# Attention with column norms and a soft mixture of experts: five products of ones in place of nine, a first load in three parts, and a new order of all steps

## The chip, the cores and the metric

The kernel runs on one core of one Trainium2 chip. The metric is device time in microseconds (us), the median of several runs. The engines are named as in the profile: PE is TensorE (PEld its weight loads), DVE is VectorE, ACT is ScalarE, POOL is GpSimd, SP is SyncE, which issues all loads and stores here.

## The reference, cut to what matters

```python
B, N, C = 4, 5056, 256                      # q, k, v: [B, N, C], float32
qn = q / (norm(q, axis=1) + 1e-6)           # a norm for each column, over the N rows
kn = k / (norm(k, axis=1) + 1e-6)
s = kn.transpose(0, 2, 1) @ qn / tau        # [B, C, C]: channels by channels
a = softmax(s, -1)
x = (v @ a).reshape(B * N, C)               # 20224 rows
logits = x @ phi                            # 8 experts of 4 slots: 32 columns
d = softmax(logits, 0)                      # over all 20224 rows
slot_in = d.T @ x                           # [32, C]
slot_out[e] = relu(slot_in[e] @ w1[e]) @ w2[e]   # F = 1024
out = softmax(logits, 1) @ slot_out         # [20224, C]
```

## The kernel before

The work comes in 40 units of 512 rows of q and k (`raw0` to `raw39`, ten for a batch, each one load of 1 MB by `load_qk`), 20 pairs of row blocks of v (`v0` to `v19`, five for a batch, 1 MB each), and the weights.

For each unit, PE sums k^T q of its four row blocks (j = 0 to 3, 128 rows each) into a bank of PSUM, `S0` to `S3` for the four batches (`score`, line 255). A half of a unit (two of the four blocks) is done in one of two ways. Plain, it is four products with float32 operands; the trace records a float32 product as two pieces, so that these are eight records, with the operand named `raw`. Split, if it stands in the table `SPLIT`, ACT first makes a rounded copy (`cast`, line 204), DVE the rest that the rounding left (`low`, line 209), both into a buffer `hl<unit>_<half>`, and PE does twelve quicker products on these. Of each row block the first product needs the cast alone, the second the rest too. For the norms ACT squares each unit (`square`, line 220) and DVE adds the squares up (`add`, line 235).

When a batch is summed, its norms and its softmax are worked out and folded with phi into a matrix `M<batch>`. Logits `L<pair>` (line 403) are products of v, turned so that channels lie on the partitions, with M. Turned v (`x<pair>`, two halves by channel) is either loaded turned from a second copy in memory (`load_vt`; the pairs and halves of the table `LT`), or made by PE from v (`turn`, line 376, into a bank `vTp<pair>_<block>_<half>`) and copied by ACT (`turned`, line 381). `G` (line 503) gathers v by the weights of the dispatch softmax. All this is interleaved with the later units' sums.

After the last unit comes a tail: the slots' inputs are joined over batches (`gs`, `gt`, `slp`, lines 518 to 621), the experts run (`H`, line 677; a transposition `hTp`, line 693, copied to `hT`; `O`, line 711), and each output block is a product (`op`, line 750) of the flipped softmax weights (`lg`, flipped by DVE, line 651) with the slots' outputs, copied out of PSUM by ACT and DVE (lines 772 and 774) and stored in 25 stores.

The order of all this is written out by hand: the program first makes a list of 992 steps and then emits them in the order of the table `ORDER`. Every engine does its instructions in the order of emission. Big buffers are 22 places of SBUF, assigned by the table `HOME`; a load into a place waits until its last reader is done.

At the very start DVE writes a tile of ones, and PE multiplies it with itself `WAKE` times (`wake`, line 787), ahead of its first product on loaded data; each is two records. The first load is line 167.

Of the kernel before, what the change touches and what calls it, by code (L numbers as in the profile page):

```python
# [20 lines left out]
WAKE = 9  # L21
PITCH = 128
NU = B * UB
NRAW = 5
MIX = (UB - 1, 3 * UB - 1)
SPLIT = {(u, 0) for u in range(1, NU) if u not in (1, 2, 3, 17, 20, 27, 31)} | {(u, 1) for u in (2, 5, 14, 24, 26, 27, 31, 33, 35, 37, 39)}
LT = {(p, 0) for p in (0, 2, 3, 4, 5, 6, 7, 8, 9, 11, 12, 13, 15, 18, 19)} | {(p, 1) for p in (0, 3, 6, 9, 12, 15)}
GR = {b: (3, 2) for b in range(B)}
HOME = {
# [74 lines left out]
def colnorm_attention_soft_moe(  # L104
# [59 lines left out]
    def load_few():  # L164
        sp.dma_start(few_sb, few)

    load_qk(0, ((0, 1), (1, 4)))
    for u in range(1, NRAW):
        load_qk(u)

# [623 lines left out]

    at(-2, wake, WAKE)
    FV = 13
    for u in range(NU):
# [3 lines left out]
        for k in range(2):  # L801
            if (u, k) in SPLIT:
                at(u - 1.08, cast, u, k)
# [292 lines left out]
```

## Time and profile before

| | |
|---|---|
| median of 3 runs | 277.36 us (277.16 to 277.69) |
| profiled execution, its own time | 277.06 us |
| its span in the trace | 275.3 us |
| PE busy | 254.6 us, 92% of the span |
| DVE busy | 236.8 us, 86% |
| ACT busy | 195.5 us, 71% |
| moved by the DMA queues | 111.44 MB, of them 20.97 MB written |

The span is what the profiler saw between the first and the last instruction; 1.76 us of the execution's own time lie outside it. The shares are averages over three different stages: the units (to about 200 us), the join and the experts (to about 217 us), and the output.

### The profile page before, as it was taken

The numbers are of one execution on the slowest core, as the hardware profiler recorded it, in microseconds if no ns is written. First come the engines' busy times: TensorE is split into PE (matmuls) and PEld (weight loads), VectorE is DVE, ScalarE is ACT, GpSimd is POOL, SyncE is SP. The second block draws the span as 40 slices with busy tenths as digits, with TensorE's granted clock in tenths as the row PEclk, the third lists the DMA queues.
The fourth block names the chain that finished last, engine by engine and source line by source line (L and its number), as shares of the span: only waits on it lengthen the run. The fifth ranks groups of instructions, "written<-read, shape, count | busy, mean of one in ns | idle before, by whom it ended". The sixth has DMA issues, their size and how long they took to land.

```text
span 275.3 us, 6127 instructions
## 1 busy us (share of the span) xinstructions
PE 254.6 (92%) x2494; PEld 212.6 (77%) x2494; DVE 236.8 (86%) x349; ACT 195.5 (71%) x285; POOL 7.5 (3%) x12
## 2 busy tenths in 40 slices
PE   8999999999999999999999999999999988678730
PEld 8889998999998896997898978866555878457520
DVE  1599999999999999999999997887989879988630
ACT  3898989798899689899998783886416247353430
POOL 1000002000002000020000001000000000000000
PEclk9999999999999999999999999999999999855755
DMA  7999999999999999999999999999999789999995
GB/s 283 432 424 410 422 426 415 420 417 419 419 417 420 412 422 421 416 415 417 412 419 418 416 417 419 417 416 420 421 415 420 300 332 388 418 418 412 420 421 246
DMA packets 17883, 111.44 MB, mean 405 GB/s; under 512 B 2112, under 2 KB 2112, under 8 KB 6592
## 3 DMA queue, kind: packets, MB, share of 16 engines
q1 hardware_dynamic: 17856, 111.06, 98.0%
q8 instruction: 19, 0.31, 0.4%
q14 instruction: 8, 0.07, 0.1%
HBM read 90.08 MB, written 20.97 MB: 403 GB/s over the span
## 4 chain that ended last, share of the span: by engine, by line
PE 87%; DVE 6%; ACT 3%; issue 1%; DVEq 0%; ACTq 0%
PE S L255 46%; PE op_None L750 8%; PE L L403 7%; PE G L503 7%; PE vTp L376 6%; PE op L750 3%; PE O L711 2%; DVE o L774 2%; ACT o L772 2%; PE wake L787 2%; PE Mp L347 1%; PE nn L266 1%; DVE nat L630 1%; DVE cm L627 1%; PE sp L549 1%; PE gt L525 1%
## 5 line engine op out<-in xcount | busy, mean ns | idle before, releaser
L235 DVE TENSOR_TENSOR sq<-sq,sq 128x1024 f32<-128x1024 f32 (+1 forms) x61 | 81.3, 1356 | 8.4 <-ACT sq L220 8.0
L220 ACT ACTIVATE sq<-raw 128x2048 f32<-128x2048 f32 (+1 forms) x40 | 74.7, 1889 | 6.5 <-DMA raw<-in_qk_dram 4.8
L255 PE MATMUL S<-hl 128*128 128x256 f32 x516 | 71.5, 291 | 0.0
L255 PE MATMUL S<-raw 128*128 128x256 f32 (+1 forms) x296 | 66.9, 384 | 0.0
L255 PEld LDWEIGHTS S<-hl 128*128 128x128 f32 x516 | 65.2, 191 | 1.0
L255 PEld LDWEIGHTS S<-raw 128*128 128x128 f32 (+1 forms) x296 | 53.7, 192 | 8.1 <-issue 1.5
L209 DVE TENSOR_TENSOR hl<-raw,hl 128x1024 fp32r<-128x1024 f32 x43 | 51.6, 1219 | 0.7 <-ACT hl L204 0.7
L204 ACT CAST hl<-raw 128x1024 fp32r<-128x1024 f32 x43 | 44.0, 1048 | 6.1 <-PE S L255 2.5
L750 PE MATMUL op_None<-so,lg 32*128 32x256 f32 x240 | 26.4, 525 | 6.0 <-ACT o L772 4.1
L772 ACT COPY o<-op_None 128x512 f32<-128x512 f32 x30 | 15.8, 594 | 18.2 <-PE op_None L750 17.9
L750 PEld LDWEIGHTS op_None<-so,lg 32*128 32x128 f32 x240 | 19.6, 251 | 11.6 <-ACT o L772 6.3
L381 ACT COPY x<-vTp 128x512 f32<-128x512 f32 x38 | 21.5, 593 | 9.3 <-PE vTp L376 8.8
L774 DVE COPY o<-op_None 128x512 f32<-128x512 f32 x30 | 19.0, 678 | 8.0 <-PE op_None L750 8.0
L376 PE MATMUL vTp<-ident,v 128*128 128x128 f32 x152 | 21.6, 276 | 0.0
L403 PE MATMUL L<-x,M 128*32 128x256 f32 (+1 forms) x320 | 20.3, 379 | 0.0
L376 PEld LDWEIGHTS vTp<-ident,v 128*128 128x128 f32 x152 | 17.3, 143 | 2.8 <-issue 2.5
L503 PE MATMUL G<-v,dn 128*32 128x256 f32 x320 | 19.1, 381 | 0.0
L503 PEld LDWEIGHTS G<-v,dn 128*32 128x32 f32 x320 | 10.8, 110 | 5.9 <-issue 0.7
L403 PEld LDWEIGHTS L<-x,M 128*32 128x32 f32 x320 | 9.8, 109 | 6.2 <-issue 0.8
L750 PE MATMUL op<-so,lg 32*128 32x128 f32 x160 | 9.6, 315 | 2.0 <-ACT o L772 1.4
L750 PEld LDWEIGHTS op<-so,lg 32*128 32x128 f32 x160 | 7.7, 197 | 4.4 <-ACT o L772 2.7
L772 ACT COPY o<-op 128x256 f32<-128x256 f32 x20 | 6.4, 378 | 6.3 <-PE op L750 6.3
(112 smaller groups left out, 233.0 us busy)
## 6 DMA issues: line engine op xcount, KB each, us to landing
raw<-in_qk_dram SPq DMA_DIRECT2D x37, 1024.0 KB, 12.5
v<-in_v_dram SPq DMA_DIRECT2D x20, 1024.0 KB, 11.1
w<-in_moe_w_dram SPq DMA_DIRECT2D x16, 1024.0 KB, 17.5
out_dram<-o SPq DMA_DIRECT2D x15, 1024.0 KB, 7.5
x<-in_vt_dram SPq DMA_DIRECT2D x17, 512.0 KB, 10.2
out_dram<-o SPq DMA_DIRECT2D x10, 512.0 KB, 3.7
raw<-in_qk_dram SPq DMA_DIRECT2D x3, 768.0 KB, 10.0
x<-in_vt_dram SPq DMA_DIRECT2D x4, 480.0 KB, 11.9
```

Source lines behind the costliest of these rows:

```text
L204: act.copy(hl[:, :, 0::2, :], raws[u][:, 2 * k : 2 * k + 2])
L209: dve.tensor_tensor(hl[:, :, 1::2, :], raws[u][:, 2 * k : 2 * k + 2], hl[:, :, 0::2, :].bitcast(F32), op=ALU.subtract)
L220: act.activation(sq_tile(u)[:, :n], raws[u][:, :n], AF.Square)
L235: dve.tensor_tensor(a[:, lo:hi], a[:, lo:hi], s[:, lo:hi], op=ALU.add)
L255: pe.matmul(sm, w, x, start=first[bb], stop=False, skip_group_check=True)
L376: pe.transpose(tp[:, P * jj : P * jj + P], vs[p][:, 4 * h + jj, P * m : P * m + P], ident)
L381: act.copy(x[:, h * UT : h * UT + UT], tps[p, h, m])
L403: pe.matmul(L[S * g : S * g + S, :n, :], M[:, m, :], x[:, :n, S * g : S * g + S], start=m == 0, stop=m == 1,)
L503: pe.matmul(gp[S * g : S * g + S, :C], dn[:, x, j, :], vt[:, j, :], start=x == 0 and j < G, stop=x == n - 1 and j >= G,)
L750: pe.matmul(ops[b, p, hf, g][:, h, :], cT[b][S * g : S * g + S, 4 * i : 4 * i + 4, :].rearrange("s j t -> s (j t)"), so[S * g : S * g + S] ...
L772: act.copy(dst, src)
L774: dve.tensor_copy(dst, src)
```

## The change

`WAKE` goes from 9 to 5. The first load, unit 0, comes in three parts (block 0, block 1, blocks 2 and 3) in place of two (block 0, blocks 1 to 3). The table `SPLIT` has 41 halves in place of 43: six are gone (the second half of unit 5, the first halves of units 4, 13, 22, 23 and 25), four are new (the first halves of units 1 and 31, the second halves of units 19 and 25). In `LT` the first channel half of pair 1 is now loaded turned, and that of pair 18 is turned on PE. `HOME` and `ORDER` are new throughout. The program's text is otherwise the same; its line numbers are lower by one from line 100 on.

```diff
-WAKE = 9
+WAKE = 5
...
-SPLIT = {(u, 0) for u in range(1, NU) if u not in (1, 2, 3, 17, 20, 27, 31)} | {(u, 1) for u in (2, 5, 14, 24, 26, 27, 31, 33, 35, 37, 39)}
-LT = {(p, 0) for p in (0, 2, 3, 4, 5, 6, 7, 8, 9, 11, 12, 13, 15, 18, 19)} | {(p, 1) for p in (0, 3, 6, 9, 12, 15)}
+SPLIT = {(u, 0) for u in range(1, NU) if u not in (2, 3, 4, 13, 17, 20, 22, 23, 25, 27)} | {(u, 1) for u in (2, 14, 19, 24, 25, 26, 27, 31, 33, 35, 37, 39)}
+LT = {(p, 0) for p in (0, 1, 2, 3, 4, 5, 6, 7, 8, 9, 11, 12, 13, 15, 19)} | {(p, 1) for p in (0, 3, 6, 9, 12, 15)}
...
-    "raw0": 0, "raw1": 1, "raw2": 2, "raw3": 3, "raw4": 4, "sq0": 5, "sq1": 6, "sq2": 8, "hl2_1": 7, "sq3": 18,
...
+    "raw0": 0, "raw1": 1, "raw2": 2, "raw3": 3, "raw4": 4, "sq0": 5, "sq1": 7, "hl2_1": 8, "sq2": 9, "hl1_0": 6,
...
-    1, 7, 14, 18, 0, 2, 3, 5, 4, 9, 12, 11, 20, 10, 21, 28, 6, 13, 38, 29, 634, 22, 113, 135, 49, 76, 8, 15, 23, 30,
...
+    1, 7, 11, 16, 20, 25, 32, 8, 12, 17, 21, 26, 33, 0, 2, 5, 3, 4, 13, 14, 10, 9, 23, 22, 30, 19, 18, 35, 27, 6,
...
-    load_qk(0, ((0, 1), (1, 4)))
+    load_qk(0, ((0, 1), (1, 2), (2, 4)))
```

Three places show what this does to the engines' orders. A row is one group of instructions as they stand on the engine: line, operation, the tile written and the tiles read (with a buffer number), the shape, and how many.

The first place is the start of the program. PE before:

```order
L787 MATMUL wake_120<-ones_88 128x128 x9
L255 MATMUL S0_130<-raw0_72 128x256 x8
L255 MATMUL S0_130<-raw1_75 128x256 x6
L255 MATMUL S0_130<-raw2_77 128x256 x2
L255 MATMUL S0_130<-raw1_75 128x256 x2
L255 MATMUL S0_130<-raw2_77 128x256 x2
L255 MATMUL S0_130<-raw3_79 128x256 x6
```

PE with the change, at the same place:

```order
L786 MATMUL wake_133<-ones_89 128x128 x5
L254 MATMUL S0_139<-raw0_72 128x256 x8
L254 MATMUL S0_139<-raw1_76 128x256 x4
L254 MATMUL S0_139<-hl1_0_115 128x256 x12
L254 MATMUL S0_139<-raw2_78 128x256 x4
L254 MATMUL S0_139<-raw3_80 128x256 x2
L254 MATMUL S0_139<-hl2_1_119 128x256 x12
```

Unit 1's first half is now done split, as the third group after the ones; before, the first split half was that of unit 2, after units 1, 2 and 3 had all been begun plainly. On DVE, which makes the rest that such a half needs, before:

```order
L187 COPY fold4_98<-fold_96 128x32 x4
L235 TENSOR_TENSOR sq0_112<-sq0_112,sq1_114 128x2048
L209 TENSOR_TENSOR hl2_1_116<-raw2_77,hl2_1_116 128x4x256
L235 TENSOR_TENSOR sq0_112<-sq0_112,sq2_118 128x2048
L235 TENSOR_TENSOR sq0_112<-sq0_112,sq3_174 128x2048
```

and with the change:

```order
L186 COPY fold4_99<-fold_97 128x32 x4
L208 TENSOR_TENSOR hl1_0_115<-raw1_76,hl1_0_115 128x4x256
L234 TENSOR_TENSOR sq0_113<-sq0_113,sq1_117 128x2048
L208 TENSOR_TENSOR hl2_1_119<-raw2_78,hl2_1_119 128x4x256
L234 TENSOR_TENSOR sq0_113<-sq0_113,sq2_121 128x2048
```

The rest of unit 1 now stands ahead of the first addition of squares.

The second place is on PE around the logits of pairs 5 to 7, in the middle of the program. Before:

```order
L503 MATMUL G0_1_1200<-v3_961,dn0_1_1182 32x256 x8
L503 MATMUL G0_1_1200<-v4_607,dn0_1_1182 32x256 x8
L403 MATMUL L5_1217<-x5_1040,M1_1194 32x256 x8
L403 MATMUL L6_1226<-x6_1056,M1_1194 32x256 x8
L376 MATMUL vTp8_1_1_1259<-ident_83,v8_1060 128x128 x4
L255 MATMUL S3_1063<-hl33_1_1116 128x256 x6
L255 MATMUL S2_501<-hl27_1_1179 128x256 x6
L525 MATMUL gt0_1276<-ident_83,gs0_1118 128x128 x2
L376 MATMUL vTp8_0_1_1279<-ident_83,v8_1060 128x128 x4
L255 MATMUL S2_501<-hl27_1_1179 128x256 x6
L403 MATMUL L7_1290<-x7_959,M1_1194 32x256 x8
L255 MATMUL S3_1063<-raw32_953 128x256 x2
```

With the change:

```order
L502 MATMUL G0_1_1151<-v3_965,dn0_1_1073 32x256 x8
L402 MATMUL L5_1160<-x5_969,M1_1145 32x256 x8
L402 MATMUL L6_1169<-x6_973,M1_1145 32x256 x8
L502 MATMUL G0_1_1151<-v4_580,dn0_1_1073 32x256 x8
L402 MATMUL L7_1214<-x7_971,M1_1145 32x256 x8
L375 MATMUL vTp8_1_1_1223<-ident_84,v8_976 128x128 x4
```

`L7` stood by itself and now stands with the others. Counted over the whole of PE's order, unbroken runs of L and G are 14 before and 13 with the change.

The third place is on DVE in the output stage, where it flips the weights (`lg`) and copies output blocks. Before:

```order
L774 COPY o0_0_2505<-op0_0_0_1_2493 128x256
L774 COPY o0_0_2505<-op0_0_0_3_2495 128x256
L774 COPY o0_4_2523<-op0_4_0_1_2511 128x256
L774 COPY o0_4_2523<-op0_4_0_3_2513 128x256
L651 STREAM_TRANSPOSE lg3_106<-nat3_2201 128x768
L723 COPY ob1_2574<-O1_2416 128x128
```

With the change:

```order
L773 COPY o0_0_2478<-op0_0_0_1_2467 128x256
L773 COPY o0_0_2478<-op0_0_0_3_2469 128x256
L650 STREAM_TRANSPOSE lg3_107<-nat3_2173 128x512
L773 COPY o0_4_2531<-op0_4_0_1_2493 128x256
L773 COPY o0_4_2531<-op0_4_0_3_2495 128x256
L650 STREAM_TRANSPOSE lg2_106<-nat2_2241 128x768
L722 COPY ob1_2550<-O1_2391 128x128
```

Two flips now stand ahead of `ob1` where one did. Not shown: PE does the transposition `hTp1_1` ahead of `hTp1_0` with the change, and the other way round before.

## Rows read from the trace of the kernel before

**Rows 1.** Stretches: length, busy us of PE, PEld, DVE, ACT, POOL (instructions), granted clock, DMA share, GB/s.

```profile
20.00:100.00 80.00, 80.00 (x562) 73.55 (x561) 78.93 (x83) 70.49 (x70) 4.30 (x3) 1.00 1.01 418
216.00:222.00 6.00, 5.63 (x127) 4.04 (x118) 4.49 (x10) 2.21 (x7) 0.00 (x0) 1.00 0.66 268
222.00:230.00 8.00, 7.48 (x182) 6.66 (x180) 6.40 (x16) 4.28 (x14) 0.00 (x0) 1.00 0.83 333
230.00:235.00 5.00, 4.26 (x62) 3.66 (x55) 5.00 (x8) 2.80 (x6) 0.00 (x0) 1.00 1.03 407
```

**Rows 2.** Chain that ended last, its head: start us, us, what.

```profile
1.04 4.21 PE wake L787 x18
5.25 38.77 PE S L255 x222
```

**Rows 3.** Instructions of line 787, and of line 255 at two early stretches: duration ns min/median/max.

```profile
L787 PE MATMUL wake<-ones x18: 421/421/582, 1.0 to 4.8; 128*128 128x128 f32 x18
...
L255 PE MATMUL S<-raw x3: 634/634/634, 5.0 to 5.9; 128*128 128x256 f32 x3
...
L255 PE MATMUL S<-raw x12: 379/379/380, 6.6 to 9.0; 128*128 128x256 f32 x12
```

**Rows 4.** First loads: the two parts' issues with us to landing, then raw1 and raw2.

```profile
raw<-in_qk_dram SPq DMA_DIRECT2D x1, 768.0 KB, 4.4
raw<-in_qk_dram SPq DMA_DIRECT2D x1, 256.0 KB, 2.6
...
L146 SPq DMA_DIRECT2D raw<-in_qk_dram x3: 421/424/432, 1.2 to 2.1; - x3
...
DMA to landing us min/median/max: 4.4/6.4/8.4
```

**Rows 5.** ACT in order of time at the start: start us, us, what [idle before].

```profile
5.65 1.91 ACT L220 ACTIVATE sq<-raw 128x2048 f32<-128x2048 f32 x1 [3.43 <-DMA raw<-in_qk_dram]
8.07 1.91 ACT L220 ACTIVATE sq<-raw 128x2048 f32<-128x2048 f32 x1 [0.51 <-DMA raw<-in_qk_dram]
10.55 1.05 ACT L204 CAST hl<-raw 128x1024 fp32r<-128x1024 f32 x1 [0.57 <-DMA raw<-in_qk_dram]
```

**Rows 6.** DVE in order of time at the start: the first rest of a split half.

```profile
12.22 1.22 DVE L209 TENSOR_TENSOR hl<-raw,hl 128x1024 fp32r<-128x1024 f32 x1
```

**Rows 7.** Chain that ended last, six pieces of PE from its middle: start us, us, what.

```profile
73.33 1.43 PE S L255 x12
...
79.29 1.73 PE S L255 x8
...
160.50 1.00 PE L L403 x16
...
163.23 0.86 PE L L403 x16
164.10 0.59 PE vTp L376 x4
...
167.50 0.44 PE vTp L376 x4
```

**Rows 8.** PE in order of time, experts' stage: the one idle time between H and O.

```profile
212.03 1.16 PE L693 MATMUL hTp<-ident,hs 128*128 128x128 f32 x8 [0.18 <-ACT hs L687]
```

**Rows 9.** PE in order of time in the output stage.

```profile
241.63 2.27 PE L750 MATMUL op<-so,lg 32*128 32x128 f32 x16 [1.15 <-ACT o L772]
243.76 2.09 PE L750 MATMUL op_None<-so,lg 32*128 32x256 f32 x16
246.78 3.38 PE L750 MATMUL op_None<-so,lg 32*128 32x256 f32 x16 [0.93 <-ACT o L772]
250.97 5.28 PE L750 MATMUL op_None<-so,lg 32*128 32x256 f32 x48 [0.81 <-DVE lg L651]
```

**Rows 10.** Stretches of one us in the output stage, columns as in Rows 1.

```profile
254.00:255.00 1.00, 1.00 (x14) 0.86 (x12) 1.00 (x2) 0.25 (x1) 0.00 (x0) 0.50 1.05 438
255.00:256.00 1.00, 1.00 (x16) 0.84 (x11) 0.70 (x2) 0.00 (x0) 0.00 (x0) 0.69 0.97 401
256.00:257.00 1.00, 0.48 (x8) 0.24 (x2) 0.65 (x2) 0.87 (x2) 0.00 (x0) 1.00 0.98 410
```

129 rows, old and new, of tables (HOME, ORDER) are left out of this document.

## The prediction, made before the changed kernel ran

> **What bounds the kernel now.** I read the table of stretches first. From 20 to 100 us PE is busy all of the time, DVE nearly (78.9 of 80 us), and the DMA share is 1.01 [rows 1]. PE, DVE and the transfers are therefore all close to their limit, and the chain of waits has to say which ends last: it runs on PE from 1.04 us, first over the ones and then over the sums S, without a stop [rows 2]. So up to the tail, time that PE saves or loses moves the end, as long as no load and no DVE result comes to stand in its way. Behind the tail's chain come the stores, and there the DMA share is 0.66 and 0.83 in two stretches before it is full again [rows 1]. These gaps mean that the transfers could take an earlier start of the output without a collision.
>
> **The start.** The eighteen records of the ones take 4.21 us [rows 2], 0.234 each, so ten of them take 2.34 and end at 3.38. The first part of unit 0 is issued at about 0.73 and lands after 2.6 us [rows 4], at 3.33; ACT began 0.1 after its own load had landed (1.15 + 4.4 = 5.55 against 5.65) [rows 4, 5]. PE can therefore start S at 3.43 in place of 5.05, 1.6 us sooner. What is this worth? The first S records take 634 ns and start 0.427 apart (three from 5.0 to 5.9), and from 6.6 on they take 379 ns and start 0.2135 apart [rows 3]. That is the step between the two levels of PE's clock, 1.2 and 2.4 GHz, and it falls at about 6.3 us, after 5.3 us in which PE had worked without a break. If it still falls at 6.3, S runs 2.87 us at the low level in place of 1.27 and does 3.75 records more by then, which would later have taken 0.2135 each: **-0.80 us**, half of what the start moves.
>
> For this the second block must be there when PE has done the first one's four records, at 5.14. In the old load it came with a part that landed at 5.55. Now it is a part of 256 KB; the 768 KB took 2.22 us to follow the first part, so a third of them lands at about 4.1. That cover is ample, and without it PE would lose 0.5. The third issue takes SP another 0.42 us [rows 4], but unit 1 lands 6.4 and unit 2 8.4 us after issues that are 0.42 apart, which is the pace of the transfers, not of the issues: unit 1 stays at 8.07 as ACT saw it [rows 5]. PE ends unit 0 at 6.3 + 9.25 x 0.2135 = 8.29, so it doesn't wait there.
>
> **The new split half.** After unit 0 PE does eight plain records of unit 1 (1.71), to 10.00, and then the half that was made split. ACT is free at 7.56 and casts from 8.07 for 1.05 us [rows 5]; DVE's rest takes 1.22 [rows 6] and ends at about 10.4. The first of the twelve products needs only the cast and ends at 10.12; the second waits to 10.45: **+0.33 us**. Behind it on PE stand all sums. The ends are 0, if PE comes later for another reason, and 0.45. The next such half (of unit 2) is ready at 14.4, when PE comes to it.
>
> **Fewer split halves.** Twelve split records take 1.43 us, eight plain ones 1.73 [rows 7]: 0.30 for a half, and two fewer are split, **+0.60 us**. DVE is rid of two rests of 1.22, ACT of two casts of 1.05. This gives PE nothing directly, since it doesn't wait for them after the start; it pays only by making later results punctual.
>
> **Order.** L after S costs 1.00 for 16 records, after G 0.86; turning costs 0.59 right after L and 0.44 otherwise [rows 7]. A visit to these narrow products therefore costs some 0.29, and there is one fewer: **-0.29 us**. With the transposition of the second expert group turned round, PE need not stand idle for 0.18 before it [rows 8]; the copies behind it could take part of this back, so I take **-0.10** (0 to -0.18). The other moved steps (places of buffers, the order of loads, eight turns that go from pair 1 to pair 18, with their two copies on ACT) keep their number of instructions, and the bytes loaded are the same. Their price is where PE meets a result at the very moment: G of pairs 0 to 2 with its flipped weights, logits of pair 5 with M1, the turns of pair 16 in a bank that ACT has just copied out, M3 behind a copy of x18. By adding up the rows of each engine I find five such places, with 0.1 us or less at each. Nothing excludes zero, and all five would be 0.5: I take **+0.20**, nearer to zero, since before PE shows no such wait.
>
> The sum is -0.80 + 0.33 + 0.60 - 0.29 - 0.10 + 0.20 = -0.06 us. The profiled execution took 277.06 us, which makes 277.0; the median of the runs is 0.30 above it, so the forecast for the median is **277.3**, no change. What a measurement tells from no change is about 0.2%, 0.55 us.
>
> **Rival 1: the clock rises later (slower).** The ones now end close to the moment when the load lands, and a pause of up to 0.2 us stands between them and S; before, there was none. The output stage shows what a break can do: PE worked from 241.6 to 245.9 and from 246.8 to 250.2 at the low level, each followed by an idle time of 0.8 to 0.9, and only after 250.97, in work without a stop, did the granted clock go from 0.50 to 1.00, in the slice from 255 to 256, 4.6 us later [rows 9, 10]. If the short pause has the same effect, the level rises 4.6 to 5.3 us after 3.43, at 8.0 to 8.7 in place of 6.3, and costs half of 1.7 to 2.4, 0.85 to 1.2; the wait of 0.33 at the split half then vanishes, since PE comes later. Net +0.5 to +0.9, time 277.8 to 278.1. It decides as soon as the rise moves by more than 1.8 us. Against it: those pauses were four times as long, and from 230 to 235 PE idled for 0.74 us with the granted clock still at 1.00 [rows 1]. The Trainium skill, "TensorE: Matmul & The Clock Gate", section "What's actually happening", says that recent activity releases the throttle, whatever the number of products, and that the moment of release moves from run to run. By this four fewer products need not delay it; the rows above agree that a release follows work without a stop, and none shows a short pause ahead of one. Chance 0.18.
>
> **Rival 2: new waits on PE (slower).** With PE and DVE both full, an order in which a handful of results come 0.2 to 0.3 late in place of 0.1 gives +1.0 to +1.5 in place of +0.20: 278.1 to 278.6. For it: every step was moved, and DVE has one free us in 80. Against it: DVE has 2.4 us less to do. Chance 0.10.
>
> **Rival 3: the third part delays the loads (slower).** At the pace of 418 GB/s [rows 1], 256 KB take 0.63 us, and the first part took 2.6 [rows 4]: if these 2 us were paid again for one more part, unit 1 would come at 10.05, PE would wait for it from 8.3 (+1.75), the split half's wait would grow from 0.33 to 0.55, and the time would be 279.3. The landings 2 us apart after issues 0.42 apart speak against it. The Trainium skill, "DMA: Bandwidth & Descriptors", section "Rules for kernel authors", advises at least 1 MiB in a transfer, and few large ones rather than many. Chance 0.02.
>
> **Rival 4: the output fills its gaps (faster).** From 222 to 230 the transfers idle for 17% of 8 us, 1.36 us, and from 230 on the share is full [rows 1]: there the end is set by stores, and what is stored sooner in the gap comes off the end. One flip of batch 3 now stands ahead of two copies of batch 0. If this lets the third batch's output start soon enough to fill half of the gap, 0.7 us go, and the time is 276.6; with none of the small waits 276.4. Against it: PE is busy for 7.48 of these 8 us, so it has little to give sooner. Chance 0.20.
>
> **How the numbers follow.** The forecast has 0.50: its terms leave -0.5 to +0.5 around it, 276.8 to 277.8, nearly all within 0.2%. Rival 1 lies at the bound and mostly over it. Faster is rival 4 alone, 0.20; slower is rivals 1 to 3 less 0.03 that stay within, 0.27; the rest, 0.53, is the same. The range from 276.5 to 278.3 leaves out most of rival 2, rival 3 and the edge of rival 4, some 0.15.
>
> **What will show it.** Right: the ones end near 3.4, the first S records run from 3.4, those of 634 ns end near 6.3, PE waits about 0.3 for DVE near 10.1 us and for nothing else up to 200, and the join's `gs` starts within 0.3 of 200.10. The start is wrong if the long records go on beyond 7; the order is wrong if the waits show PE idle for DVE or ACT between 12 and 200; and rival 4 holds if the first stores leave at the old time and the DMA share from 222 to 230 is above 0.9. The forecast as a whole fails if a load lands after PE asks for it, which the margins of several us after the first five units make unlikely.

## The result, and the profile after

The changed kernel takes 280.47 us (median of 6 runs, 279.83 to 281.80) against 277.26 for the kernel before: a ratio of 1.0116, 95% interval 1.0083 to 1.0149. It is slower by 3.2 us, where no change was forecast. The profiled execution has a span of 278.9 us, 3.6 more than before.

The chain of waits of the changed kernel shows where it begins: start us, us, what.

```profile
1.64 5.96 DMA raw<-in_qk_dram
7.60 0.04 issue
7.64 37.76 PE S L254 x194
...
200.74 0.42 PE join L562 x2
```

The third part of unit 0, issued at 1.64, ends at 7.60, and only then does the chain go on with S. Before, S ran from 5.25 on without a wait [rows 2]. The join of the batches, the first step of the tail, stood here in the chain before:

```profile
196.88 0.42 PE join L563 x2
```

So at the join 3.86 us have been lost, 3.6 of which are left at the end. PE in order of time at the start of the changed kernel:

```profile
1.05 2.50 PE L786 MATMUL wake<-ones 128*128 128x128 f32 x10 [1.05 <-DVE half L175]
3.43 2.07 PE L254 MATMUL S<-raw 128*128 128x256 f32 x4
7.64 7.21 PE L254 MATMUL S<-raw 128*128 128x256 f32 x20 [2.15 <-DMA raw<-in_qk_dram]
14.51 1.78 PE L254 MATMUL S<-hl 128*128 128x256 f32 x12
```

The first S record starts at 3.43, as forecast. Four records later PE stands for 2.15 us until blocks 2 and 3 are there, and the records that follow are long. Block 1 had landed by then (1.17 + 2.9 = 4.1 us, below), but it is not PE's next one: step 0 of the list is the ones, steps 2 to 5 are the blocks of unit 0, and `ORDER` has 0, 2, 3, 5, 4 before and 0, 2, 5, 3, 4 with the change. PE took the blocks as 0, 1, 3, 2, and now takes them as 0, 3, 1, 2. Line 254 in two stretches (9 to 11 us, and 13.6 to 14.2):

```profile
L254 PE MATMUL S<-raw x6: 634/634/634, 8.7 to 10.8; 128*128 128x256 f32 x6
...
L254 PE MATMUL S<-raw x4: 379/379/379, 13.4 to 14.0; 128*128 128x256 f32 x4
```

634 ns is the length at PE's low level, 379 that at the high one [rows 3]: the level rises only near 13, where before it rose near 6.3. The 24 records ahead of the first split half end at 14.5. By the steps of [rows 3], 24 records ended at 5.05 + 3 x 0.427 + 21 x 0.2135 = 10.8 before. The loss of the start is thus 3.7 us, where 0.80 had been forecast as a gain.

The loads themselves: us from issue to landing, of the first three issues and of the first four.

```profile
DMA to landing us min/median/max: 2.7/2.9/6.0
...
DMA to landing us min/median/max: 2.7/4.4/8.0
```

The two parts of 256 KB land after 2.7 and 2.9, the part of 512 KB after 6.0, unit 1 after 8.0, at 10.06 in place of 7.97. Stretches of 2 us, columns as in [rows 1], of the changed kernel, and then of the kernel before:

```profile
2.00:4.00 2.00, 2.00 (x9) 1.75 (x8) 0.18 (x3) 0.21 (x2) 0.00 (x0) 1.00 0.83 276
4.00:6.00 2.00, 1.50 (x4) 0.67 (x2) 0.00 (x0) 0.00 (x0) 0.00 (x0) 1.00 0.73 217
6.00:8.00 2.00, 0.35 (x1) 0.36 (x2) 0.00 (x0) 0.29 (x1) 0.00 (x0) 1.00 0.98 375
```

```profile
4.00:6.00 2.00, 2.00 (x9) 1.82 (x9) 0.00 (x0) 0.35 (x1) 0.00 (x0) 1.00 1.02 426
```

From 4 to 6 us the transfers move half of what they moved before, with loads queued behind them. (The column of the granted clock reads 1.00 here though the records are long; in this stretch the records tell the level, not this column.)

### The profile page after: what moved, and what is told of

It reads as the page before. It is cut to its first block, busy times and chain, and to the rows that moved or that the text cites. A ratio compares the mean times of both kernels' runs of the same rounds, so it can differ in the third digit from the quotient of the medians.

```text
span 278.9 us, 6082 instructions
## 1 busy us (share of the span) xinstructions
PE 255.5 (92%) x2478; PEld 213.2 (76%) x2478; DVE 235.5 (84%) x347; ACT 194.0 (70%) x283; POOL 8.3 (3%) x12
## 4 chain that ended last, share of the span: by engine, by line
PE 85%; DVE 4%; DMA 3%; ACT 2%; issue 1%; SPq 0%; DVEq 0%; ACTq 0%
PE S L254 46%; PE L L402 7%; PE G L502 6%; PE vTp L375 6%; PE op_None L749 6%; PE O L710 3%; DVE o L773 3%; PE H L676 3%; DMA raw<-in_qk_dram 2%; ACT o L771 2%; PE op L749 2%; PE Mp L346 1%; PE nn L265 1%; DMA out_dram<-o 1%; PE sp L548 1%
## 5 line engine op out<-in xcount | busy, mean ns | idle before, releaser
L254 PE MATMUL S<-raw 128*128 128x256 f32 (+1 forms) x312 | 73.4, 395 | 2.1 <-DMA raw<-in_qk_dram 2.1
L254 PE MATMUL S<-hl 128*128 128x256 f32 x492 | 68.0, 292 | 0.0
L254 PEld LDWEIGHTS S<-raw 128*128 128x128 f32 (+1 forms) x312 | 58.5, 198 | 11.7 <-DMA raw<-in_qk_dram 3.0
L254 PEld LDWEIGHTS S<-hl 128*128 128x128 f32 x492 | 62.2, 191 | 1.0
L208 DVE TENSOR_TENSOR hl<-raw,hl 128x1024 fp32r<-128x1024 f32 x41 | 48.9, 1215 | 9.0 <-ACT hl L203 9.0
L203 ACT CAST hl<-raw 128x1024 fp32r<-128x1024 f32 x41 | 42.0, 1046 | 5.8 <-issue 2.8
L502 PE MATMUL G<-v,dn 128*32 128x256 f32 x320 | 20.0, 380 | 0.0
L502 PEld LDWEIGHTS G<-v,dn 128*32 128x32 f32 x320 | 12.2, 110 | 4.7 <-issue 0.7
L275 POOL TENSOR_TENSOR rn<-rn,half 128x4 f32<-128x4 f32 x4 | 6.6, 1660 | 151.9 <-DVE rn L270 108.6
L749 PE MATMUL op<-so,lg 32*128 32x128 f32 x160 | 7.7, 296 | 1.9 <-ACT o L771 1.2
## 6 DMA issues: line engine op xcount, KB each, us to landing
x<-in_vt_dram SPq DMA_DIRECT2D x17, 512.0 KB, 10.4
```

Of the source, the lines that this page charges most:

```text
L203: act.copy(hl[:, :, 0::2, :], raws[u][:, 2 * k : 2 * k + 2])
L208: dve.tensor_tensor(hl[:, :, 1::2, :], raws[u][:, 2 * k : 2 * k + 2], hl[:, :, 0::2, :].bitcast(F32), op=ALU.subtract)
L254: pe.matmul(sm, w, x, start=first[bb], stop=False, skip_group_check=True)
L502: pe.matmul(gp[S * g : S * g + S, :C], dn[:, x, j, :], vt[:, j, :], start=x == 0 and j < G, stop=x == n - 1 and j >= G,)
L749: pe.matmul(ops[b, p, hf, g][:, h, :], cT[b][S * g : S * g + S, 4 * i : 4 * i + 4, :].rearrange("s j t -> s (j t)"), so[S * g : S * g + S] ...
```

## The experiments

Three theories were put to the test: A, the third part delays all loads and breaks PE's work; B, fewer ones alone keep the clock low; C, the new order costs. The start's two edits were first undone in the changed kernel, one at a time and together, and the third part alone was put into the kernel before.

**The changed kernel, first load in two parts.**

```diff
-    load_qk(0, ((0, 1), (1, 2), (2, 4)))
+    load_qk(0, ((0, 1), (1, 4)))
```

> The changed kernel (280.5 us) with one edit: the first load in two parts again, five ones kept. Theory A (the third part): in the changed kernel's trace its 512 KB landed 6.0 us after their issue, at 7.6, and every later load came 2 us late. Without it unit 0 is complete at 5.65 and unit 1 at 8.07, PE waits 0.5 us for blocks 1 to 3 (5.14 to 5.65), and the time falls to 276.5 if the clock still rises near 6.3 or to 278.5 if it rises 5.3 us after the work resumes. Theory B (the pause alone: after five ones PE is not busy long enough, whatever the parts): no change, 280 or more, with long S records to 13. Theory C (the new order of steps is what costs): also no change, 280 or more, but with short records from 7 on and waits of PE later.

278.02 us (10 runs), ratio to the kernel before 1.0022 (1.0004 to 1.0041). The kernel before stood at 277.35 beside this run and the next three. This gives back 2.45 of the 3.2 us; B and C said none. A had 276.5 for an early rise of the clock, and the rise was early (below): 1.5 us of that did not come. PE in order of time:

```profile
3.42 1.60 PE L254 MATMUL S<-raw 128*128 128x256 f32 x4
5.59 4.58 PE L254 MATMUL S<-raw 128*128 128x256 f32 x20 [0.57 <-DMA raw<-in_qk_dram]
9.82 2.15 PE L254 MATMUL S<-hl 128*128 128x256 f32 x12
11.81 2.75 PE L254 MATMUL S<-raw 128*128 128x256 f32 x12
```

and line 254 of the same kernel from 3 to 5.2 us:

```profile
L254 PE MATMUL S<-raw x4: 379/478/795, 3.4 to 4.6; 128*128 128x256 f32 x4
```

After five ones, with short pauses ahead of S and at 5.0, the level rose at about 4.3: the records are short by 4.6. That refutes B for this trace. The twelve split records take 1.99 us to the next row where they take 1.62 without a wait (14.51 to 16.13 in the changed kernel): the forecast wait of the new split half is there, 0.37.

**The changed kernel, nine ones.**

```diff
-WAKE = 5
+WAKE = 9
```

> The changed kernel with one edit: nine products of ones again, three parts kept. Theory A: the third part still lands at 7.6 and PE waits about 0.9 us for it after four records of each of blocks 0 and 1, unit 1 comes at 10.1; but PE has worked without a break from 1.04 to 6.7, so the clock rises at 6.3 as in the kernel before, and 2 to 2.7 us come back: 277.8 to 278.5. Theory B: the cover is all that was missing: 277.3. Theory C: 279.5 or more.

280.12 us (10 runs, 278.09 to 282.29), 1.0077 (1.0051 to 1.0103): above A's range, in C's. Yet its start, PE in order of time, is much as A has it, but for the wait, which is 1.58 us after four records where A had 0.9 after eight:

```profile
5.04 1.31 PE L254 MATMUL S<-raw 128*128 128x256 f32 x4
7.93 4.58 PE L254 MATMUL S<-raw 128*128 128x256 f32 x20 [1.58 <-DMA raw<-in_qk_dram]
12.16 2.19 PE L254 MATMUL S<-hl 128*128 128x256 f32 x12
```

and the join in its chain of waits:

```profile
199.55 0.42 PE join L562 x2
```

The clock had risen before the wait and stayed up, so the 24 records end at 12.16, 2.35 us sooner than in the changed kernel. But at the join only 1.19 of this is left. The loads are still 2 us late, and PE now meets DVE's rests: the split half takes 2.03 us to the next row where it takes 1.62 in the changed kernel, and at 32 us PE waits 0.50 for another rest. This A had left out. Behind the join, PE stands for 1.32 us at one place of this trace (below).

**The changed kernel with both edits of the start undone** (the two diffs above together), three times.

> The changed kernel with both edits of the start undone (nine ones, two parts): the new tables of split halves, turned loads, buffers and order alone. Theories A and B: the start is that of the kernel before, what is left is +0.60 for two more plain halves, -0.29 for a visit less and the small terms: 277.3 to 278.0. Theory C: 279 or more, and the trace shows where PE waits after 12 us.

> The new tables and order with the start of the kernel before, once more, for its trace. Its time had a wide spread (277.0 to 280.6, median 278.9), and its first trace was the fastest of these, where the end came 0.1 us before that of the kernel before although the join of the batches stood 0.40 later. Theory C' (the tail of the new order loses time in most executions): a time near 279 with the join at 197.3 as before and the loss behind it: the product H of the experts at PE's low level (6.9 for 5.3 us, as in two traces of the old order of 279 us) or waits in the output. Theory of the units (loads or DVE late in some executions): the join later than 198.

> The same kernel a third time, with the same two readings: the loss of a slow execution lies behind the join (C'), or before it.

The timed runs: 278.88 us (12 runs, 276.98 to 280.63), 1.0044 (1.0018 to 1.0069), between the two expected ranges. The joins of the three traces stand at 197.28, 197.29 and 197.42, the start in these differing by up to 1.07 us (24 records end at 11.06, 10.63 and 9.99). So the tables and the order cost 0.40 to 0.54 up to the join, and an earlier start of PE is swallowed before it: in the first trace PE waits nowhere, in the others 0.18 and 0.51 us for a rest of DVE near 30 us. Two of the traces end with a span of 275.2 and 275.5, like before; the third took 281.26 us. Its chain behind the join:

```profile
217.96 0.43 PE op L749 x7
218.39 1.56 issue
219.95 1.00 PE op L749 x9
220.95 1.01 PE O L710 x16
221.96 1.17 PE op L749 x16
```

and the same place in the first trace:

```profile
217.81 0.43 PE op L749 x7
218.24 0.13 issue
218.37 0.59 PE op L749 x9
218.96 0.57 PE O L710 x16
219.53 0.66 PE op L749 x16
```

PE waits for nothing that the profile names, 1.56 us long in place of 0.13, and then everything takes nearly twice as long; the stretch from 220 to 222 us of the third trace has the low level:

```profile
220.00:222.00 2.00, 2.00 (x29) 1.36 (x29) 1.17 (x3) 0.65 (x2) 0.00 (x0) 0.50 0.03 8
```

This is C' of the expectation, in its second form (the output), and that execution ends 4.3 us after the first, of which the join has 0.14. In the trace with nine ones the same gap is 1.32 us, without a fall of the clock.

**The kernel before with the third part, with five ones, and with both.**

```diff
-    load_qk(0, ((0, 1), (1, 4)))
+    load_qk(0, ((0, 1), (1, 2), (2, 4)))
```

```diff
-WAKE = 9
+WAKE = 5
```

> The kernel before (277.3 us) with one edit: its first load in the three parts of the change. Theory A: the last part lands at about 7.6 and units 1, 2, 3 at 10.1, 12.5, 15; PE waits about 0.9 for the last part and 0.7 for unit 1, the clock rises at 6.3 nevertheless; 278.3 to 279.3. If the parts are harmless (theories B and C): 277.3, with unit 1 at 8.1.

> The kernel before (277.3 us) with five ones, its first load in two parts as it was. PE starts S at 3.4, does four records and waits for blocks 1 to 3 until 5.6. If the two short pauses don't hold the clock back (as in the run of the changed kernel with two parts, where short records began near 4.3): unit 0 ends at 8.2 in place of 9.1, and 0.3 to 0.9 us are won, 276.4 to 277.0, or nothing if PE meets the loads of units 1 to 4 later. If the pauses do hold it back to 10.9 (rival 1 of the prediction): 24 records end 1.8 later, 279.

> The kernel before with the whole start of the change (five ones, three parts), its tables and order kept. Theory A (the third part makes the last part land near 7.6 and breaks PE's work, so that the clock rises only near 13): nearly all of the slowdown, 279.5 to 280.3. If the new order were needed for it: 278.7, as with three parts and nine ones.

The third part alone: 278.66 us (10 runs), 1.0055 (1.0031 to 1.0078), as A expected. PE waits for the part and then for unit 1:

```profile
8.16 1.99 PE L255 MATMUL S<-raw 128*128 128x256 f32 x8 [1.47 <-DMA raw<-in_qk_dram]
10.64 10.63 PE L255 MATMUL S<-raw 128*128 128x256 f32 x48 [0.49 <-DMA raw<-in_qk_dram]
```

Its join stands in the chain at

```profile
199.03 0.42 PE join L563 x2
```

Five ones alone: 278.21 us (10 runs, 276.62 to 278.56), 1.0014 (0.9987 to 1.0042), no change that can be told. Its join is at 196.72, 0.16 earlier than before: at 36 us PE waits 0.33 for a load, where before it waited for none. Both: 278.77 us (10 runs, 277.60 to 280.47), 1.0048 (1.0016 to 1.0080). This misses A's 279.5 to 280.3: in the trace the clock had risen near 5.2, ahead of the wait of 0.92 us for the third part, and stayed up through it. A had counted on a low level after every such break. PE in order of time:

```profile
3.39 3.04 PE L255 MATMUL S<-raw 128*128 128x256 f32 x8
7.35 1.99 PE L255 MATMUL S<-raw 128*128 128x256 f32 x8 [0.92 <-DMA raw<-in_qk_dram]
```

In the old order PE has eight records to do, those of blocks 0 and 1, before it needs the third part, so its wait is 0.92 where the changed kernel's is 2.15. Its join is at 198.05, 1.17 after that of the kernel before and 0.98 ahead of that with three parts and nine ones.

**The changed kernel again.**

> The changed kernel again. Theory A with a clock that rises at another moment in every execution: the third part lands at 7.3 to 8.1 again and PE waits for it. If the clock has risen ahead of this wait (near 4 to 5.5, as in four traces of the variants) short S records follow from the end of the wait on, and the join comes near 199.5; if not, long records to about 13 and the join near 200.7 as in the first trace.

280.68 us. PE waited 2.50 us, until 8.07, and the join came at 200.21. Line 254 from 8 to 9 and from 9.7 to 11 us:

```profile
L254 PE MATMUL S<-raw x4: 379/444/617, 8.1 to 8.8; 128*128 128x256 f32 x4
...
L254 PE MATMUL S<-raw x5: 634/634/634, 9.2 to 10.9; 128*128 128x256 f32 x5
```

The first records after the wait are short and those after 8.7 long, to 11.8: the level had risen and fell again behind the idle time. Neither of the two cases expected: after this break PE runs a second stretch at the low level. In the experts' stage this execution loses 1.7 us more, with the product H at 7.05 us where the kernel before has 5.36:

```profile
206.00 7.05 PE L676 MATMUL H<-w,slT 128*32 128x512 f32 x48
```

**What about the parts it is.** Five other cuts of units 0 and 1, in the kernel before. Each is one edit of the line of the first load or the lines behind it:

```diff
-    load_qk(0, ((0, 1), (1, 4)))
+    load_qk(0, ((0, 2), (2, 4)))
```

> The kernel before with its first load in two parts of 512 KB (blocks 0 and 1, blocks 2 and 3). A look at what makes the third part dear. If it is the number of parts: the second part lands near 5.6 and unit 1 near 8.0, 277.3. If it is the short rows of a part (4 KB for a partition, where the 768 KB part has 6 KB): the second part lands after 6.5 and unit 1 after 9, 278 or more.

```diff
     load_qk(0, ((0, 1), (1, 4)))
-    for u in range(1, NRAW):
+    load_qk(1, ((0, 2), (2, 4)))
+    for u in range(2, NRAW):
```

> The kernel before with its first load as it was and unit 1 loaded in two parts of 512 KB in place of one of 1 MB. If every further load among the first costs 2 us of the transfers: unit 1 complete at 10, unit 2 at 12.5, 278.5. If only short parts right behind the first one do: unit 1 complete near 8.1, 277.3.

```diff
-    load_qk(0, ((0, 1), (1, 4)))
+    load_qk(0, ((0, 1), (1, 3), (3, 4)))
```

> The kernel before with its first load in three parts of another cut: block 0, blocks 1 and 2, block 3 (256, 512 and 256 KB in place of 256, 256 and 512). If three parts of one unit are the reason for the lost transfers: the last part lands after 7 and unit 1 near 10. If two short parts one right behind the other are: the last part near 5.7 and unit 1 near 8.1.

The other two cut unit 1 into `((0, 1), (1, 2), (2, 4))` with unit 0 as before, and unit 0 into four single blocks.

> The kernel before, its first load in two parts as it was, unit 1 loaded in three parts (256, 256 and 512 KB). If three transfers into one tile are what delays: the last part of unit 1 lands near 10 and unit 2 near 12.5. If only the first unit's transfers matter, with which the stream starts: unit 1 complete near 8.1 and unit 2 near 10.5.

> The kernel before with its first load in four parts of 256 KB. If every part beyond the second costs 2 us of the transfers: the last part lands near 9.5 to 10 and unit 1 near 12. If the loss is one of the start as such, whatever the number: the last part near 8 and unit 1 near 10, as with three.

us from issue to landing in each, of the first issues up to that of the unit behind the cut one (the maximum is its own). Halves of unit 0, three issues, the last one (unit 1) at 1.6:

```profile
DMA to landing us min/median/max: 3.7/4.5/6.5
```

Halves of unit 1, five issues, the last (unit 2) at 2.6:

```profile
DMA to landing us min/median/max: 2.7/5.2/8.0
```

256, 512 and 256 KB of unit 0, four issues, the last (unit 1) at 2.1:

```profile
DMA to landing us min/median/max: 2.6/5.0/8.3
```

Unit 1 in three, six issues, the last (unit 2) at 3.1:

```profile
DMA to landing us min/median/max: 2.6/4.9/7.9
```

Unit 0 in four, five issues, the last (unit 1) at 2.6:

```profile
DMA to landing us min/median/max: 2.7/4.0/7.2
```

So with halves of unit 0, unit 1 comes at 8.1, no loss there. With halves of unit 1, unit 2 comes at 10.6, with thirds of it at 11.0: 0.1 and 0.5 later than before (2.1 + 8.4, [rows 4]). With the other cut into three, unit 1 comes at 10.4, the loss again; with four parts at 9.8, the loss once, not twice. It is neither rows of 4 KB nor further loads as such, but more than two parts in the first unit, with which the stream of transfers starts, and it is paid once. With four blocks, more than two parts also means at least two parts of 256 KB, so these runs can't tell the number of parts from two such short ones. Why the transfers slow down is not settled: no view shows what they wait for.

The single times of these five (279.06, 279.14, 278.32, 278.63, 278.60 us) say little of the cuts. With three and four parts of unit 0 the joins came at 198.2 and 198.9. With the other three cuts they came at 197.5, 0.6 later than before: there PE waits 0.85 to 0.98 us for a load at 22 us, for which it did not wait before, and up to 1.6 us more go in the product H. Whether the cut or the execution brings these two is not shown. With halves of unit 0:

```profile
22.21 1.99 PE L255 MATMUL S<-raw 128*128 128x256 f32 x8 [0.95 <-DMA raw<-in_qk_dram]
...
203.28 6.99 PE L677 MATMUL H<-w,slT 128*32 128x512 f32 x48
```

## Why the prediction was wrong, by its own steps

**The step that failed is in the start:** "unit 1 lands 6.4 and unit 2 8.4 us after issues that are 0.42 apart, which is the pace of the transfers, not of the issues: unit 1 stays at 8.07", and with it the cover of the last two blocks. What the third part cost was not its issue but transfer time: the last blocks came at 7.6 in place of 5.6 and unit 1 at 10.06. In the new order with nine ones, that moves the join by 2.27 us (197.28 to 199.55), in the old one by 2.15 (196.88 to 199.03), and in the old one with five ones by 1.33 (196.72 to 198.05).

**A second step that failed** stands beside it: "For this the second block must be there when PE has done the first one's four records". The block came at 4.1, as forecast, but in the new order PE needs block 3 there, which is in the last part in either cut. So the part for block 1 saves no wait in this order. Even with the last part at its old time PE would stand for some 0.5 us, as it does with two parts (0.57); with the part at 7.6 it stands after four records, not after eight.

**Rival 3** had this mechanism, its place and its size (unit 1 at 10.05, about 2 us), and got a chance of 0.02, since landings behind two parts were taken to tell of landings behind three. That the size agrees is in part luck: its reason, 2 us again for one more part, would make four parts dearer than three, and they are not. The Trainium skill, "DMA: Bandwidth & Descriptors", section "Rules for kernel authors", advises few large transfers; the traces agree for three and four parts of the first unit, and not for two parts of 512 KB, which cost the landing of unit 1 nothing.

**The clock** was held at one moment, 6.3 us. In the traces whose PE worked on, it rose anywhere from before 4.8 (three parts in the old order) to 6.8 (256, 512 and 256 KB), with the same nine ones, as line 255 shows in the first of these,

```profile
L255 PE MATMUL S<-raw x1: 382/382/382, 4.8 to 4.8; 128*128 128x256 f32 x1
```

and in the second:

```profile
L255 PE MATMUL S<-raw x4: 634/634/634, 5.5 to 6.8; 128*128 128x256 f32 x4
```

Of this spread the Trainium skill says in "TensorE: Matmul & The Clock Gate", section "What's actually happening", that the moment moves from run to run, by 0.5 us either way; the traces agree that it moves, and show at least 2 us from the earliest to the latest. So -0.80 was no fixed gain: in both orders, five ones with two parts bring the join 0.16 to 0.17 earlier, and no time that these runs can tell. Rival 1 named a pause as the danger, but the wrong one: the short one ahead of S, or 0.57, 0.92, 1.47 and 1.58 us after a rise, did nothing. Those of 2.15 and 2.50, which began while the records were still long, did, and put the steady high level off to about 13 and 12; whether their length or the level before them decides is not shown. Together with the ones taken away, the third part therefore costs 3.63 at the join (197.11 to 200.74) in place of 2.27 in the new order. In the old order it is the other way round, 1.33 in place of 2.15: the wait of 2.15 us needs the late part, the early start of S, and a block order that leaves PE only four records to do. That interplay was in no case of the prediction. The part of the block order in it is argued from the place of the wait; no run changed that order alone.

**The split half** was right in size: 0.37 against 0.33, in the run with two parts. In the changed kernel itself PE came after 14 us and met no wait, as the step's lower end said.

**The order** was forecast at 0.60 - 0.29 + 0.20 = +0.51 up to the join, and is 0.40 to 0.54. Rival 2's small waits did not come in the changed kernel: from 14.5 to 200 us its chain shows PE without a pause. With two parts or nine ones, where PE is earlier, one of 0.18 to 0.51 us for DVE came near 30 us in four of five traces. But the timed runs of the order alone say 1.0044, 1.2 us, with a spread of 3.7 us. One trace of that shows the gap of 1.56 us and the low level behind it; that this explains the other long times too is argued, not shown.

**Rival 4** came in part. From 222 to 230 us the share was 0.66 in the changed kernel, against 0.83 [rows 1], but the changed kernel is then at an earlier stage, since its join is 3.86 late. Four us later it has

```profile
226.00:234.00 8.00, 7.48 (x172) 6.66 (x169) 7.56 (x18) 4.95 (x15) 0.00 (x0) 1.00 0.88 352
```

and the new order with the start of before has 0.88 from 222 to 230: more than 0.83, less than the 0.9 that was named as its sign. From the join to the end of the span the changed kernel takes 78.2 us and the kernel before 78.4, so next to nothing came of it.

The parts, as joins of single traces: order +0.40, third part +2.27, five ones on top of it +1.19, together the 3.86 that were lost. The timed runs share the 3.2 us out less sharply, with intervals of some 0.7 us either way: order 1.2 (1.0044), third part 0.9 more (1.0077), five ones 1.1 more (1.0116). By the way of two parts it is order and five ones 0.6 (1.0022) and then the third part 2.6; in the old order the third part is 1.5 (1.0055), and on top of five ones 0.9 (1.0048 against 1.0014), which the intervals don't set apart from nothing. So the third part is the largest cost, 2.6 of the 3.2 us where it alone is taken out of the changed kernel; how the rest is shared between the order and the ones is not settled by the times. No version of the parts beats the kernel before: the nearest is that with five ones alone, which is the same.

## What to carry to other kernels

Where the transfers run at their limit from the start, most of what the first loads lost was still missing at the join (1.3 to 2.3 us, where unit 1 came 1.7 to 2.6 late), and of the 1.6 us that PE won at the start 0.16 or 0.17 were left; read the landing times of all first loads before cutting one of them. Before pricing a smaller first part, look up which part the engine needs next: a part that comes early is worth nothing if the order asks for another. An edit of one start condition (cover for the clock) is safe only as long as the other (no break in the work behind it) holds: price them together. A landing time read behind two transfers does not tell of three.

## What the runs showed of the hardware

More than two parts in the first unit cost 1.7 to 2.6 us of the landing of unit 1, once, with three cuts of it and in both orders; two parts, or parts of the second unit, cost the landing of the next unit 0.5 or nothing.

PE's level can fall within the experts' stage (H 6.99 and 7.05 us in place of 5.36) or in the output, in some executions of the same program and not in others. With halves of unit 0 it fell near 203.2, as H began, behind 2 us in which PE was busy for 1.76:

```profile
201.00:203.00 2.00, 1.76 (x15) 1.76 (x15) 1.30 (x8) 0.00 (x0) 0.00 (x0) 1.00 0.95 397
...
203.50:205.00 1.50, 1.50 (x10) 0.21 (x6) 1.50 (x2) 0.07 (x1) 0.00 (x0) 0.50 1.02 410
```

The kernel before is busy for 1.77 of the same 2 us, and its level stays up.

With the same nine ones, the level rises at the start between before 4.8 and 6.8 us.

PE stood for 0.13 to 1.56 us for nothing that the profile names, behind the seventh record of the first output product (the new order with nine ones). With five ones it stands behind the fifteenth (0.23 in the changed kernel, 0.91 with two parts): eight records later, where eight records of ones are gone. So its place goes with the count of PE's records, not with what they work on. In the trace with 0.13 one transfer of the instruction queue ran between 215 and 216 us, in that with 1.56 between 217 and 218. That PE waits there for code fits all of this, and is not shown. The Trainium skill, "Runtime: NRT & Kernel Launch", section "Instruction fetch mechanics", says that a sequencer fetches its next block while it runs the current one, mostly hidden; the trace with 0.13 agrees, that with 1.56 would not if the fetch is what it waits for, and no run here took the fetch away.
